# Two of four batches get their queries by rows of a block, turned by transposing transfers, with a second set of row-order tables

## The chip, the core and the metric

The kernel runs on one core of one Trainium2 chip. The metric is the device time of one execution in microseconds; the median of the runs shown is the time of the kernel. One execution was also profiled, and all rows below are of that one.

## What is computed

```python
# q, k, v: [4, 8, 768, 64]; sort_net: [4, 8, 8, 8]; w_ch1: [512, 2048]; w_ch2: [2048, 512]
for _ in range(5): P = exp(P - max); P /= P.sum(-1); P /= P.sum(-2)      # sinkhorn
k_sorted = einsum('bhij,bhjcd->bhicd', P, k_blocks)                      # 8 blocks of 96 tokens
v_sorted = einsum('bhij,bhjcd->bhicd', P, v_blocks)
attn = softmax(q_block @ k_sorted_block.T / 8)                           # inside a block
x = (attn @ v_sorted_block) as [4, 768, 512]
u = x + real(fft(fft(x, axis=1), axis=2))
un = (u - mean) / sqrt(var + 1e-6)
out = u + relu(un @ w_ch1) @ w_ch2                                       # "MLP"
```

## The kernel before

Four batches pass through the same stages. **Mix**: for each of four pairs of heads `hp`, queries and keys are loaded by POOL (`load_kq`; the transfer also turns them to 16 bits). Partition p of a loaded tile holds six neighbouring tokens, so a block's 96 tokens stand in an order of their own, `PERM`. TensorE turns the queries (`q_mix`: twelve matmuls with the identity, L800, and a copy out of PSUM to `qT` by DVE or ACT); twelve more mix the keys (`k_mix`, L821, evicted to `kz`). From batch 1 on the two sets are one step, `psQK`. The values are mixed (L761), written to `vo` and moved by SP to `vs` (`v_move`, L783).

**Attention**: per pair and half of the blocks `y`, scores (`products`, L853), a maximum or minimum on DVE, `exp` on ACT, then the product with the values (L937) and a division on DVE to `xr`. In batches 2 and 3 (`turned`) the probabilities come out with queries on the partitions and are turned by a transposing transfer on SP's queue (`turn_e`, L912), two per half.

**Fourier transform**: sums and differences of blocks (`fold`), a matmul with the tables `cse` and `cso` over the tokens of a block (`dft_s`, L983, L1005, out to `W`), a matmul over the model dimension (`dft_d`, L1045), and `residual` (L1088) with a selection matrix `rsel`. The rows of `cse`, `cso` and `rsel` stand in the order of the queries in a block. All three are loaded once, by SP.

**Norm and MLP**: `PQ`, `u`, statistics (L1115), `un`, transposes into `unT` (by TensorE in batch 0, L1162, by SP's transposing transfers later, L1153), then the MLP's matmuls: L1180 (`ph`, 128 groups of four) and L1198 (`pc`, 96 groups of four).

A planner, `Plan`, sets the order on every engine. Each step has a cost per engine, a due time (moved by the tables `LEAD` and `MOVE`) and, if it ends in a transfer, `work` and `hop`; `SPARE` is added to a transfer's landing. The order is fixed when the kernel is built: each engine runs its own list and waits where an input is late. Into gaps of TensorE's list before the planned time `FILL_END` it puts matmuls that nobody reads (`fill`, L687). Loads for batches 2 and 3 are held back by one-element copies on POOL (`landed`, L493), which wait for an earlier load.

Of the kernel before, what the change touches and what calls it, by code (L numbers as in the profile page):

```python
# [28 lines left out]
TURN = 8  # L29
# [31 lines left out]
def _consts():  # L61
# [21 lines left out]
    ss = BLK * np.arange(4)[None, :] + PERM[:, None]  # L83
# [39 lines left out]
    at = np.argsort(PERM)  # L123
# [84 lines left out]
class Plan:  # L208
    FORM_IN = dict(psQ=1, psK=1, psQK=1, psaT=1, psS=2, psRh=5, psM=6)
    FORM_OUT = dict(FORM_IN, psT=2)  # L210
    ENTER, LEAVE, STAY = 0, 95, 1e7
    ARRAY = dict(psQ=320, psK=320, psQK=640, psaT=53, psS=155, psA=213, psB=213, psT=395, psV=160, psN=159, psWo=510,
        psWe=271, psF=430, psR=324, psRh=162, psY=213, ph=640, pc=853, psG=640, psP=60, pcol=60)
    FILL_LOW, FILL_END, WINDOW = 1931, 49895, 3413
    LAG, PE_TAIL, MARGIN, NEAR = 45.0, 250.0, 120.0, 14.0
    PORT, PORT_WAIT = ("fold", "fold_d", "minus", "nm", "un", "xem", "kron"), 450.0
    OVER = {"V": 80, "A": 100}
    SPARE = 909
    REL = dict(cdh=38223, cse=17364, cso=12887, idx=43588, load_k2=82421, load_k3=45767, load_q1=32871,
        load_q2=83959, load_q3=155044, load_v1=26759, load_v2=99397, load_v3=18886, rsel=30643, w0=38071,  # L220
        w1=51566, w2=7303, w3=34666, w4=62534, w5=56660, w6=23527, w7=18919)
    LEAD = dict(P=(-10.9, -33.1, 10.8, 47.7), Q=(-21.5, 0, 0, -19.8), We=(-1.6, -0.2, 0.2, 0),
        Wo=(24.9, -10.8, 0, -20.3), a16=(-11.2, -16.6, 1.4, 0), a_out=(26.9, 10.9, 36.1, -20.1),
        add=(-68, 0, 74.6, -10.9), amr=(0.9, 2.6, 18, 0), amt=(-58.6, -2.5, -4.5, 0), const=(15.9, 0, 0, 0),
        exp=(10.9, 48.2, 35.7, -8.7), fold=(-27.1, -23.4, -64.4, 3.7), fold_d=(0, -4.8, 34.7, 0.1),
        hold=(-53, 0, 0, 0), kron=(2.5, 74.7, 2.1, 37.8), kz=(-20.2, 0.8, -52.6, -46.3),
        load_k16=(0, 75.7, 0, -47.8), load_q16=(0, 7.8, -23.1, -0.3), load_v=(0, 26.7, -51.4, -35.5),
        m8=(6.6, 0, 0, 0), max=(-79.4, -48, -32.6, -52.3), minus=(-40.1, -17.1, -9.6, -5.8),
        nm=(-1, -10.8, -13.3, 71.6), norm=(4.5, -39, -29.1, -35.3), ot=(43.5, 40.4, -18.7, 0),
        outt=(0, 0, -51.4, -37), patch=(3.2, 28.2, 5.1, -43.2), pc=(9.3, 0, 0, 0), pca=(19.5, 0, 0, 0),  # L230
        pcol=(-10, 0, 0, 0), pcs=(28.9, 0, 0, 0), ph=(83.6, 26, 3.3, -1.1), psA=(0, 2.4, 0, -26.9),
        psB=(7.1, 0, 2, 26.3), psF=(5.8, -0.3, 0, 19.8), psG=(71.5, 0, 0, 0), psK=(-31.8, 17.3, 37.2, 0.7),
        psM=(-45.2, 0, 0, 0), psN=(-18, -17.6, 7.4, 67), psP=(20.4, 0, 0, 0), psQ=(53.7, -3.6, 23.4, -2.4),
        psQK=(0, 8, 17.6, -16.7), psR=(-1.8, 58.2, 0, 1.6), psRh=(32.2, 16.3, 7.5, -22.1),
        psS=(47.1, 34.2, -65.3, -27.4), psT=(-29.9, -33.5, 0, 0), psV=(-64.4, 0, 24.7, -4.5),
        psWe=(-51.6, 33.5, 1.3, 0), psWo=(4.8, 37.8, 2.9, 0), psX=(26.8, 14.2, -8.8, 0), psY=(0, 25.5, 0, 0),
        psaT=(-0, -2.4, 10.7, 0.2), ptm=(-12.5, 0, 0, 0), qT=(-5.1, 0, 5.8, -57.3), relu=(1.5, 0, 9.6, 81.6),
        root=(0, 9.5, 9.1, -21.3), row_zero=(0, -26.2, -15.6, -2), stats=(-6.4, -23.2, -10.4, 1.7),
        store=(-1.5, 0, -29.6, 6.6), turn_e=(0, 0, 0, -18.6), turn_u=(0, 0, 26.1, 10.7),
        u=(37.5, 8.6, 31.2, -14.6), un=(48.6, 33.2, -20.3, -21.5), unT=(0, 62.4, 0, 15.1),  # L240
        v_move=(-23, 23.6, 0, 26.2), v_sum=(0, -10.6, 0.2, 43), vg=(65.5, 0, 0, 0),
        vo=(14.8, -41.4, -78.1, 0), weights=(62.6, 0, 0, 0), xem=(-20.9, -4.2, 0, -9),
        xom=(-38.7, 63.9, 0, 1.4))
    MOVE = dict(P={(1, 2): 15.5}, add={(2, 2): 0.8, (2, 4): 65.3, (3, 2): 44.7, (3, 4): 9.4},
        amt={(3, 0): -11.9}, const={(0, 3): -19.1},
        exp={(2, 1): 24.2, (2, 4): -13.7, (2, 5): -5.9, (2, 7): -1.2, (2, 15): -0.5, (3, 0): 6.4, (3, 5): -13.8},
        fold={(0, 3): -17.6, (0, 4): 32, (1, 3): -51.4, (2, 1): -8.6, (3, 4): 13.8}, fold_d={(2, 0): 41.8},
        kz={(3, 0): -12.5}, load_k16={(1, 1): 8.8}, minus={(3, 4): -45.6, (3, 7): -43.3}, nm={(1, 0): -20.1},
        norm={(0, 6): 6.2}, psN={(0, 4): -19}, psV={(3, 1): 0.8, (3, 2): -46.8, (3, 3): 0.9, (3, 7): -39.2},
        psWe={(0, 1): 13.5, (1, 0): 38.7, (1, 3): 15.6}, psY={(0, 2): 12.9}, relu={(0, 27): 2},  # L250
        stats={(1, 3): 41.9}, turn_e={(3, 0): 0.5}, u={(0, 2): -54.4}, un={(0, 5): -7.3},
        v_move={(1, 4): 3.2, (1, 8): 32.2, (2, 4): 2.7, (2, 6): 43.9, (2, 7): 8.4, (2, 8): 16.1, (2, 9): 44.8, (2, 11): 6.9},
        vo={(3, 0): 5.5, (3, 6): -24.1})
# [206 lines left out]
def kernel(  # L460
# [12 lines left out]
    nc.scalar.preload_act_table_set("natural_log_exp_and_others")  # L473
    names = ("small", "cdh", "cse", "cso", "vrow", "ones", "idx", "rsel")
    (small_d, cdh_d, cse_d, cso_d, vrow_d, ones_d, idx_d, rsel_d) = [
        nc.inline_tensor(a, name=n) for n, a in zip(names, _consts())]

    const = ctx.enter_context(tc.tile_pool(name="const", bufs=1))
    psum = ctx.enter_context(
# [892 lines left out]
    for b in range(B):  # L1372
        if b == 0:
            mix(0)
# [59 lines left out]
```

## Time and profile before

| | |
|---|---|
| median of 3 runs | 291.07 us (288.71 to 293.12) |
| the profiled execution | 291.53 us, span 289.7 us |
| TensorE busy | 276.1 us, 95% |
| VectorE, ScalarE, GpSimd busy | 66%, 63%, 42% |
| mean granted TensorE clock | 0.985 |
| bytes moved by transfers | 30.41 MB in 50847 packets |

The span runs from the first to the last instruction of the program. A start-to-start distance of two groups says more of TensorE than the busy time, since matmuls overlap and their ends are modelled.

### The profile page before, as it was taken

What the parts mean: (1) busy time and instruction counts of PE and PEld (TensorE: products, weight loads), DVE (VectorE), ACT (ScalarE), POOL (GpSimd) and SP (SyncE); (2) the same over time, 40 slices, a digit from 0 to 9 for tenths busy, and PEclk for the clock granted to TensorE, in tenths of its full rate; (3) what the DMA queues carried; (4) which work ended last, traced back from release to release, by engine and by line L of the source; (5) the groups of instructions that cost most, each with busy time, mean ns of one, the idle gap of its engine ahead of it and who ended that gap; (6) DMA issues with size and microseconds to landing.
All of it is one profiled execution on the core that took longest, in us unless ns stands there. A gap on an engine that the chain in (4) does not pass through costs nothing.

```text
span 289.7 us, 6877 instructions
## 1 busy us (share of the span) xinstructions
PE 276.1 (95%) x2598; PEld 161.9 (56%) x2598; DVE 191.5 (66%) x435; ACT 183.8 (63%) x455; POOL 122.0 (42%) x190
## 2 busy tenths in 40 slices
PE   7899999689999999999999999999999999999993
PEld 2467766257765565445555576455645645645541
DVE  6749988978797897673679998987866572001011
ACT  2368976778894779746495679788725832712700
POOL 8473736314226789765833256230023641112010
PEclk9979999979999999999999999999999999999998
DMA  7998969998856876969935862553311025002002
GB/s 101 182 162 169 154 106 163 185 140 136 107 88 104 112 147 96 124 143 186 130 88 113 154 112 38 115 144 75 70 38 38 36 54 129 36 34 77 1 36 74
DMA packets 50847, 30.41 MB, mean 105 GB/s; under 512 B 25962, under 2 KB 48900, under 8 KB 50812
## 3 DMA queue, kind: packets, MB, share of 16 engines
q0 software_dynamic: 19040, 19.40, 40.6%
q1 hardware_dynamic: 31574, 10.28, 18.9%
q8 instruction: 20, 0.33, 0.5%
q10 hardware_dynamic: 200, 0.30, 0.4%
q14 instruction: 13, 0.11, 0.2%
HBM read 28.50 MB, written 6.29 MB: 120 GB/s over the span
## 4 chain that ended last, share of the span: by engine, by line
PE 78%; DVE 14%; DMA 3%; issue 2%; ACT 1%; DVEq 0%
PE bank L1180 29%; PE bank L1198 24%; PE bank L983 3%; PE bank L853 3%; PE bank L937 3%; DMA eT<-es 2%; PE bank L1088 2%; PE bank L875 2%; PE bank L821 2%; PE bank L761 2%; PE bank L1005 1%; PE bank L800 1%; DVE st L1115 1%; PE bank L1045 1%; DVE mxs L863 1%
## 5 line engine op out<-in xcount | busy, mean ns | idle before, releaser
L1198 PE MATMUL bank<-w2sb,hr 128*128 128x512 f16 x384 | 90.0, 379 | 0.0
L1180 PE MATMUL bank<-unT,w1sb 128*128 128x384 f16 x512 | 89.2, 329 | 0.0
L1186 ACT ACTIVATE hr<-bank 128x384 f16<-128x384 f32 x128 | 60.7, 495 | 38.7 <-PE bank L1180 37.9
L1180 PEld LDWEIGHTS <-w1sb 128*128 128x128 f16 x512 | 49.1, 99 | 32.2 <-issue 1.5
L1219 POOL DMA_INDIRECT out_dram<-outt,idx_sb x22 | 22.6, 1026 | 88.5 <-DVE outt L1207 70.0
L1198 PEld LDWEIGHTS <-hr 128*128 128x128 f16 x384 | 36.0, 98 | 38.2
L1207 DVE SCALAR_TENSOR_TENSOR outt<-u,bank 128x512 f32<-128x512 f32 x24 | 16.4, 682 | 41.8 <-PE bank L1198 41.8
L892 ACT ACTIVATE sm<-bank,mns 96x96 f32<-96x96 f32 x128 | 32.3, 352 | 2.4 <-DVE mns L898 2.0
L944 DVE TENSOR_TENSOR xr<-bank,rz 96x512 f16<-96x512 f32 x32 | 22.0, 686 | 1.1
L547 ACT CAST W<-bank 128x384 f16<-128x384 f32 (+1 forms) x38 | 12.8, 380 | 12.9 <-PE bank L983 8.5
L1115 DVE BATCH_NORM_STATS2 st<-u 128x6 f32<-128x512 f32 x24 | 16.4, 681 | 4.0 <-POOL u L1101 3.9
L863 DVE TENSOR_REDUCE mxs<-bank 96x8 f16<-96x768 f32 x16 | 14.5, 949 | 5.6 <-PE bank L853 5.5
L1100 POOL TENSOR_TENSOR u<-u,PQ 128x257 f32<-128x257 f32 x18 | 12.8, 711 | 9.9 <-DVE PQ L1058 8.6
L898 DVE TENSOR_REDUCE mns<-bank 96x8 f32<-96x768 f32 x16 | 15.0, 944 | 2.6 <-PE bank L853 2.2
L1101 POOL TENSOR_TENSOR u<-u,PQ 128x255 f32<-128x255 f32 x18 | 12.6, 699 | 3.6 <-DVE PQ L1058 3.6
L908 ACT ACTIVATE es<-sm 96x384 f16<-96x384 f32 x19 | 10.0, 528 | 6.1 <-DMA eT<-es 5.8
L880 ACT ACTIVATE sm<-bank 96x768 f32<-96x768 f32 x16 | 12.8, 801 | 1.4 <-PE bank L853 1.2
L922 ACT ACTIVATE eT<-sm 96x768 f16<-96x768 f32 x16 | 13.4, 841 | 0.4
L569 POOL DMA_DIRECT2D k<-in_k_dram x15 | 11.0, 733 | 5.9 <-PE bank L821 4.8
L937 PEld LDWEIGHTS <-eT 97*128 97x128 f16 (+1 forms) x256 | 11.2, 101 | 3.8 <-ACT eT L922 0.5
L943 DVE RECIPROCAL rz<-bank 96x8 f32<-96x8 f32 x32 | 6.3, 197 | 10.6 <-PE bank L937 10.5
L983 PE MATMUL bank<-cso_sb,xso 120*128 120x384 f16 (+1 forms) x64 | 13.1, 326 | 0.0
(144 smaller groups left out, 426.5 us busy)
## 6 DMA issues: line engine op xcount, KB each, us to landing
vs<-vo SPq DMA_DIRECT2D x48, 65.0 KB
v<-in_v_dram POOLq DMA_DIRECT2D x16, 192.0 KB, 4.9
k<-in_k_dram POOLq DMA_DIRECT2D x15, 192.0 KB, 5.5
q<-in_q_dram POOLq DMA_DIRECT2D x15, 192.0 KB, 4.1
w1sb<-in_moe_w_ch_dram POOLq DMA_DIRECT2D x4, 512.0 KB, 8.0
w2sb<-in_moe_w_ch_dram POOLq DMA_DIRECT2D x4, 512.0 KB, 5.9
eT<-es SPq DMA_TRANSPOSE x32
cdh_sb<-cdh SPq DMA_DIRECT2D x1, 387.0 KB
```

Of the source, the lines that this page charges most:

```text
L863: ("max", b, {"V": 945}, lambda e: nc.vector.tensor_reduce(mxs[n].t.rearrange("p (t j) -> p t j", t=2), pair(pS, BLK), axis=AX.X, op=ALU.max),
L892: nc.scalar.activation(sm.t[:, i], pair(pS, BLK)[:, t, i % 4], AF.Exp, bias=mn.t[:, i:i + 1], scale=-1.0)
L898: ("max", b, {"V": 945}, lambda e: nc.vector.tensor_reduce(mn.t.rearrange("p (t j) -> p t j", t=2), pair(pS, BLK), axis=AX.X, op=ALU.min), ...
L937: nc.tensor.matmul(ps[0:wide(i).stop - BLK * i, i // 4, i % 4], et[0:97, wide(i)], vs[b % 2][:, 4 * y + i % 4, (D + 1) * h:(D + 1) * (h + 1)])
L944: nc.vector.tensor_tensor(xr2[b % 2][0:BLK, 4 * y:4 * y + 4, 128 * hp:128 * hp + 128].rearrange("p j (t d) -> p t j d", t=2), ps[:, :, :, ...
L983: nc.tensor.matmul(ps, x[0:n, j], cso[0:n, j, :], start=(j == 0), stop=(j == 3))
L1115: nc.vector.bn_stats(st.t, us[b, i, m].t)
L1180: nc.tensor.matmul(ps, w1sb[:, mc, 128 * fc:128 * fc + 128], unT[b, gr].t[:, mc, :], start=(mc == 0), stop=(mc == 3))
L1186: nc.scalar.activation(dst, bank(pH, [128, 384]), AF.Relu)
L1198: nc.tensor.matmul(ps, hr[f4].t[:, fc % 4, 128 * t:128 * (t + 1)], w2sb[:, fc, :], start=(fc == 0), stop=(fc == 15))
L1207: step("outt", b, {"V": 687}, lambda e, u=u, pC=pC, o=o: nc.vector.scalar_tensor_tensor(o.t, u.t, RSC, bank(pC, [128, DM]), op0=ALU.mult, ...
L1219: step("store", b, {"G": 1050}, lambda e: nc.gpsimd.indirect_dma_start(out=out.rearrange("b s m -> (b s) m"), out_offset=bass.IndirectOffs ...
```

## The change

For batches 2 and 3 the queries of one head are loaded as `[96 rows, 8 blocks, 64]`, so that a partition is a row of every block. Two loads fill one tile of a pair of heads, and runs of 64 elements take the place of runs of 384. Two transposing transfers on SP's queue (`turn_q`) then make `qT`; the twelve matmuls and the copy out of PSUM are gone there, and `psQK` is split. A block's queries are now in plain order in these batches, so `cso`, `cse` and `rsel` are overwritten by a second set, made with the plain order, when batch 1 has been done with them. The tile `q16` grows from 768 to 1024 elements a partition, and the ring `v16` loses one of its six tiles. `TURN` now counts batches and says the same as before.

```diff
+QT = 2
-    ENTER, LEAVE, STAY = 0, 95, 1e7
+    ENTER, LEAVE, STAY = 0, 95, 58161
-    FILL_LOW, FILL_END, WINDOW = 1931, 49895, 3413
-    LAG, PE_TAIL, MARGIN, NEAR = 45.0, 250.0, 120.0, 14.0
+    FILL_LOW, FILL_END, WINDOW = 1852, 63588, 3413
+    LAG, PE_TAIL, MARGIN, NEAR = 45.0, 250.0, 120.0, 9.0
-    SPARE = 909
+    SPARE = 630
...
-    LEAD = dict(P=(-10.9, -33.1, 10.8, 47.7), Q=(-21.5, 0, 0, -19.8), We=(-1.6, -0.2, 0.2, 0),
+    LEAD = dict(P=(-9.4, -14.6, 25.1, 1.7), Q=(0.5, 0, -0.1, 9.3), We=(25.2, -21.8, 0, 2.5),
...
-    ring("q16", 3, [128, 2, G * D], F16)
-    ring("v16", 6, [128, 2, G, D], F16)
+    ring("q16", 3, [128, NB, 128], F16)
+    ring("v16", 5, [128, 2, G, D], F16)
...
+            if b >= QT and tag == "q16":
+                for hh in range(2):
+                    step("load_q16", b, {"G": 850}, lambda e, t=d[b, hp], hh=hh: nc.gpsimd.dma_start(
+                        t.t[0:BLK, :, D * hh:D * hh + D],
+                        q[b, hs.start + hh].rearrange("(i r) d -> r i d", r=BLK)),
+                        w=[(d[b, hp], hh)], work=1500, hop=1750, bulk=2 if b > 1 else 1, need=need, rel=f"load_q{b}")
+                continue
...
+        if b >= QT:
+            for t in range(2):
+                step("turn_q", b, {"S": 1300}, lambda e, t=t: nc.sync.dma_start(
+                    qT[b, hp].t[:, 384 * t:384 * t + 384].rearrange("x (i r) -> x i r", r=BLK),
+                    q16[b, hp].t[0:BLK, 4 * t:4 * t + 4].rearrange("q i x -> q (i x)"), transpose=True),
+                    r=[(q16[b, hp], 0), (q16[b, hp], 1)], w=[(qT[b, hp], t)], work=800, hop=900)
+            return
...
+        if b == QT:
+            for key, t, d in (("cso", cso, cso2_d), ("cse", cse, cse2_d), ("rsel", rsel, rsel2_d)):
+                step("const", b, {"S": 530}, lambda e, t=t, d=d: nc.sync.dma_start(t, d.ap()),
+                     w=[key], work=6 * int(np.prod(t.shape)) // 1000 + 50, hop=1500, bulk=True, need=125e3)
```

All entries of `REL`, `LEAD` and `MOVE` are new as well, so the order changes on every engine. Over the whole program TensorE loses 96 matmuls of L800 and gains ten unread ones (18 in place of 8). Three places matter below.

**SP, from batch 1's last row copy to batch 2's first probabilities.** `qT` is the turned queries, `eT` the turned probabilities. Before:

```order
L752 DMA xr_184<-xr_184 1x16x224
L752 DMA xr_184<-xr_184 1x16x32
L912 DMA_TRANSPOSE eT_145<-es_100 128x4x96
L912 DMA_TRANSPOSE eT_146<-es_102 128x4x96
L912 DMA_TRANSPOSE eT_145<-es_101 128x4x96
```

Now:

```order
L770 DMA xr_183<-xr_183 1x16x32
L826 DMA_TRANSPOSE qT_85<-q_74 128x4x96 x2
L1402 DMA cso_sb<-cso 120x1536
L1270 DMA idx_sb<-idx 128x24
L826 DMA_TRANSPOSE qT_86<-q_75 128x4x96 x2
L1402 DMA cse_sb<-cse 120x772
L939 DMA_TRANSPOSE eT_144<-es_99 128x4x96
```

Four turns of queries and two tables stand ahead of the first turned probabilities; the third table (`rsel`) stands between later ones.

**DVE, the norm of batch 0** (`PQ` is the spectrum, `u` the sum, `st` its statistics; `vo`, `amr`, `amt`, `xso` and `xse` here are batch 1's mix). Before, from the first spectrum:

```order
L863 TENSOR_REDUCE mxs_94<-bank 96x8
L1058 TENSOR_TENSOR PQ_114<-bank,ot_113 128x258 x2
L1100 TENSOR_TENSOR u_116<-bank,PQ_114 128x257
L1101 TENSOR_TENSOR u_116<-bank,PQ_114 128x255
L1115 BN_STATS st_129<-u_116 128x6
```

Now:

```order
L558 CAST amr<-bank 128x512
L726 CAST amt<-bank 128x4x16
L727 TENSOR_TENSOR amt<-bank,amt 128x4x8
L558 CAST xso<-bank 24x4x128
L1085 TENSOR_TENSOR PQ_113<-bank,ot_112 128x258 x2
L738 COPY xse<-xso 24x8x128
L790 SCALAR_TENSOR_TENSOR vo<-a_193,bank 128x6x64 x3
L1127 TENSOR_TENSOR u_115<-bank,PQ_113 128x257
L1128 TENSOR_TENSOR u_115<-bank,PQ_113 128x255
L790 SCALAR_TENSOR_TENSOR vo<-a_193,bank 128x6x64 x2
L1085 TENSOR_TENSOR PQ_114<-bank,ot_112 128x258 x2
L1142 BN_STATS st_128<-u_115 128x6
```

Five `vo` and five small steps of batch 1 moved ahead of batch 0's statistics; they stood behind them before.

**ACT, the last batch's norm** (`ot` is the copy of an odd spectrum, `rstd` belongs to the norm; each `hr` evicts one group of four L1180 matmuls of batch 2's MLP, so its count tells how many such groups TensorE has there). Before:

```order
L547 COPY ot_113<-bank 128x258
L1186 ACTIVATE hr_66<-bank 128x384
L1075 COPY PQ_114<-bank 1x516
L1186 ACTIVATE hr_66<-bank 128x384
L1186 ACTIVATE hr_67<-bank 128x384 x4
L1186 ACTIVATE hr_68<-bank 128x384
L547 COPY ot_113<-bank 128x258
```

Now (the copies `ot` are on DVE):

```order
L1102 COPY PQ_114<-bank 1x516
L1213 ACTIVATE hr_68<-bank 128x384 x2
L1213 ACTIVATE hr_69<-bank 128x384 x3
L1151 ACTIVATE rstd_131<-mv_125,epst 128x2
L1152 ACTIVATE rstd_131<-rstd_131 128x2
L1213 ACTIVATE hr_69<-bank 128x384
```

From batch 3's first spectrum to batch 3's first MLP matmul TensorE had 16 such groups of L1180 before and has 8 now; beside them stood 13 groups of L1198 before, and stand 12 now and eight matmuls of `residual`.

107 lines of the change are left out of this document (59 added, 48 removed).

## The prediction

> **What bounds the kernel now.** I read the page first: busy time, the share of the chain that ended last, and the costliest groups.
>
> ```profile
> span 289.7 us, 6877 instructions
> ...
> PE 276.1 (95%) x2598; PEld 161.9 (56%) x2598; DVE 191.5 (66%) x435; ACT 183.8 (63%) x455; POOL 122.0 (42%) x190
> ...
> PE 78%; DVE 14%; DMA 3%; issue 2%; ACT 1%; DVEq 0%
> ...
> L1198 PE MATMUL bank<-w2sb,hr 128*128 128x512 f16 x384 | 90.0, 379 | 0.0
> L1180 PE MATMUL bank<-unT,w1sb 128*128 128x384 f16 x512 | 89.2, 329 | 0.0
> ```
>
> TensorE carries 78% of the chain, and no matmul of the MLP ever waited (idle 0.0 in both groups). An average hides stages, so next comes the table of windows of 10 us (busy time and count of PE, PEld, DVE, ACT, POOL, then the granted clock, the share of the transfer engines, GB/s).
>
> ```profile
> 50.00:60.00 10.00, 6.13 (x59) 3.69 (x58) 9.61 (x29) 7.02 (x16) 4.04 (x7) 0.96 1.06 161
> 60.00:70.00 10.00, 9.86 (x151) 6.60 (x150) 7.68 (x16) 7.74 (x15) 2.99 (x4) 0.87 0.89 133
> 100.00:110.00 10.00, 9.55 (x112) 5.95 (x111) 9.45 (x18) 8.35 (x24) 8.81 (x16) 1.00 0.83 146
> 120.00:130.00 10.00, 9.43 (x71) 4.61 (x70) 7.13 (x15) 5.16 (x18) 6.47 (x11) 1.00 0.71 141
> 250.00:260.00 10.00, 10.00 (x55) 5.13 (x53) 0.69 (x1) 3.49 (x8) 0.97 (x1) 1.00 0.00 0
> ```
>
> The two halves differ. Up to 60 us TensorE has gaps and DVE is the full engine (9.61 of 10 in 50 to 60); from the first MLP matmul on TensorE is full, with 0.14, 0.45 and 0.57 us idle in the three rows between. So the end is the time of the first MLP matmul, plus all matmul work that is left then, plus waits. An edit pays only by moving one of these three.
>
> **The transposes that go.** The order of time on TensorE shows a `psQK` step: L800 turns queries, L821 mixes keys.
>
> ```profile
> 101.17 0.53 PE L800 MATMUL bank<-ident,q 128*64 128x128 f16 x12
> 101.53 0.50 PE L821 MATMUL bank<-kron,k 128*64 128x128 f16 x12
> 101.87 0.50 PE L800 MATMUL bank<-ident,q 128*64 128x128 f16 x12
> 102.20 0.50 PE L821 MATMUL bank<-kron,k 128*64 128x128 f16 x12
> ```
>
> From start to start twelve L800 take 0.36 us (101.53 − 101.17). The busy figure, 0.53, would count the overlap twice. Eight steps go: 8 × 0.36 = **2.9 us off** a full engine, all gained. The eight copies to `qT` (on DVE or ACT) go too; I value them at nothing, since these engines are 66% and 63% busy and TensorE's MLP work covers their stages.
>
> **The ten more unread matmuls.**
>
> ```profile
> L687 PE MATMUL bank<-junk 128*128 128x512 f16 x8 | 2.6, 383 | 0.0
> ```
>
> At 0.383 us each they cost 3.8 us at most, if no gap were there. They stand ahead of 64 us of planned time, where 50 to 60 us alone had 3.87 us idle: I take nothing. They do buy clock. Rows of the chain with eight L1180 each:
>
> ```profile
> 60.70 2.27 PE bank L1180 x8
> ...
> 76.68 1.30 PE bank L1180 x8
> ```
>
> The first eight MLP matmuls took 2.27 us at a reduced clock, against 1.30 later; the window 60 to 70 was granted 0.87, that is 1.3 us of full clock lost, and 50 to 60 another 0.4, in which TensorE was partly idle. The low clock follows the window in which TensorE was busy 6.13 of 10. If the unread matmuls keep it busy, this comes back: bounds 0 (another window turns slow) to −1.7, and I take **−1.3**.
>
> **The first MLP matmul comes later.** DVE now does batch 1's five `vo`, `amr`, `amt` (two steps), `xso` and `xse` ahead of batch 0's statistics. Their prices, by form, and the gaps in DVE's order of time in the same stretch (bracketed):
>
> ```profile
> L772 DVE SCALAR_TENSOR_TENSOR vo<-a,bank 128x384 f16<-128x384 f16 x24 | 11.8, 549 | 0.5 <-PE bank L761 0.4
> L551 DVE CAST xso<-bank 24x512 f16<-24x512 f32 x2 | 1.4, 696 | 0.7 <-PE bank L713 0.7
> L720 DVE COPY xse<-xso 24x1024 f16<-24x1024 f16 x3 | 1.3, 423 | 0.4 <-ACT xso L547 0.4
> L551 DVE CAST a<-bank 128x512 f16<-128x512 f32 x1 | 0.7, 691 | 0.6 <-PE bank L695 0.6
> L708 DVE CAST amt<-bank 128x64 f16<-128x64 f32 x4 | 0.9, 219 | 0.6 <-PE bank L701 0.6
> L709 DVE TENSOR_TENSOR amt<-bank,amt 128x32 f16<-128x32 f32 x4 | 0.8, 191 | 0.1
> ```
>
> ```profile
> 43.46 1.82 DVE L863 TENSOR_REDUCE mxs<-bank 96x8 f16<-96x768 f32 x2 [0.99 <-PE bank L853]
> ...
> 46.95 0.43 DVE L1100 TENSOR_TENSOR u<-bank,PQ 128x257 f32<-128x257 f32 x1 [1.00 <-PE bank L1088]
> ...
> 49.02 0.76 DVE L1058 TENSOR_TENSOR PQ<-bank,ot 128x258 f32<-128x258 f32 x2 [0.36 <-ACT ot L547]
> ```
>
> The sum is 5 × 0.549 + 0.691 (`amr`, by the cast of the same form) + 0.219 + 0.191 + 0.696 + 0.423 = 5.0 us. The gaps hold 0.99 + 1.00 + 0.36 = 2.35 us. So the first MLP matmul comes 2.6 us (all gaps used) to 5.0 us (none) later; the middle is 3.8. Against that, TensorE now does two pairs of L800 and L821 ahead of it that stood behind it, 2 × 0.70 = 1.4 us from start to start (101.87 − 101.17), and batch 1's four short L713, together about 1.6 us of work that is no longer left then. Net +1.0 to +3.4, and I take **+2.2**.
>
> **What the transfers take.** Both queues as the page has them: packets, MB, share of 16 engines' span.
>
> ```profile
> q0 software_dynamic: 19040, 19.40, 40.6%
> q1 hardware_dynamic: 31574, 10.28, 18.9%
> ...
> q<-in_q_dram POOLq DMA_DIRECT2D x15, 192.0 KB, 4.1
> ```
>
> A q0 packet took 0.406 × 16 × 289.7 us / 19040 = 99 ns at 1019 bytes on average, a q1 packet 28 ns at 326 bytes. A pair's queries were 256 runs of 768 bytes as written; they become two loads of 768 runs of 128 bytes. One engine of 16 then needs, for a pair, 1536 / 16 × 28 to 99 ns = 2.7 to 9.5 us, against 256 / 16 × 99 = 1.6 us. Nearest in size is the q1 packet, so I take 2.7: eight pairs add 9 us of transfer time in the 120 us around batches 2 and 3. That alone is hidden, since the share there stood at 0.71 to 0.83 in the rows above and TensorE has MLP work meanwhile. POOL issues eight loads more, each under the 1 us that its issues take here, with 42% of it busy: nothing.
>
> The page "DMA: Bandwidth & Descriptors" of the Trainium skill (Specifications) says that transfers under 512 B make the engine read, modify and write. If that doubled the 28 ns, an estimate would be 5.3 us a pair, not 2.7; the average q1 packet here, at 326 bytes, shows no such price, and no row has a load in runs of 128 bytes. If it held, the second rival below would gain from it.
>
> **What waits in SP's queue.** SP issues 16 transposing transfers and three tables more. Where it is dense, the order of time shows this:
>
> ```profile
> 192.99 16.50 SPq L912 DMA_TRANSPOSE eT<-es  x11
> ```
>
> Eleven back to back in 16.50 us are 1.50 us each: SP sets the pace there. Two turns of queries now stand among batch 3's thirteen last ones, and behind each a turn of probabilities waits, and then L937. The tables wait for batch 1's last matmuls that read the old ones; behind them stand the turns of batch 2's probabilities. How late a turn can be, and how near the end is to its inputs, the chain and DVE's order show:
>
> ```profile
> 114.33 6.55 DMA eT<-es
> ...
> 218.49 1.96 PE bank L1088 x10
> 220.45 0.46 PE bank L1045 x8
> 220.91 0.86 PE bank L1198 x4
> ...
> 243.69 10.40 PE bank L1180 x64
> ```
>
> ```profile
> 241.91 0.55 DVE L1141 TENSOR_SCALAR un<-u,mv,rstd 128x512 f16<-128x512 f32 x1 [0.95 <-DMA unT<-un]
> ```
>
> One turn landed 6.55 us after its issue, and TensorE's MLP work hid it. At the end 23.2 us of other work (243.69 − 220.45) covered the way from batch 3's first spectrum to its first MLP matmul, and the fourth transpose, which that matmul needs, landed at 241.9: 1.8 us to spare. The cover now has eight groups of L1180 less (8 × 0.65 = 5.2 us), one group of L1198 less (0.9) and eight L1088 more (8 × 0.196 = 1.6): 4.5 us less. The way itself is also ordered anew, so the wait there is 0 to 4.5 − 1.8 = 2.7 us. With waits like those of 100 to 130 us (0.45 + 0.57) added once, the bounds are 0 to +3.7, and I take **+1.5**, below the middle, since the order lets ACT make three of the four `un` that DVE made in between other work.
>
> **Sum.** 291.53 − 2.9 − 1.3 + 2.2 + 1.5 = 291.0 us for a profiled execution. The profiled one stood 0.46 above the median of the runs shown, so the prediction is **290.6 us**. With the bounds of its terms (−2.9, −1.7 to 0, +1.0 to +3.4, 0 to +3.7) the likeliest case spans 287.5 to 295.3.
>
> **Rival 1, faster: the head does not get longer.** DVE's work of batch 1 falls into its gaps and into waits that the order no longer has, so the first MLP matmul comes at 60.7 us as before and 1.6 us less is left then. For it: TensorE itself stood idle 3.87 us in 50 to 60. Against: DVE was busy 9.61 of 10 in that row. Price: −2.9 − 1.7 − 1.6, and the 1.2 us idle in the three rows after 60 us vanish: −7.4, so 283.7 us by the median.
>
> **Rival 2, slower: SP's queue becomes the bound of batches 2 and 3.** Queries reach `qT` through POOL's serial loads (two per pair where one stood, each followed by a wait for an earlier one), two turns on SP, and only then come scores. For it: 1.50 us per turn in the dense stretch, a turn that took 6.55 us, `SPARE` cut from 909 to 630 ns, the cover at the end cut by 4.5 us. Against: 23 us of pure MLP cover and a TensorE list that hid all of this so far. It decides once a turn lands later than the MLP work planned ahead of its reader. Price: two more turns in the dense stretch of each batch, 2 × 2 × 1.50 = 6.0, and 2.7 at the end, on −2.9 − 1.3 + 2.2 = −2.0: +6.7, so 297.8 us.
>
> **How the numbers follow.** The likeliest case gets 0.46, rival 1 0.25, rival 2 0.29. A measurement of this kernel tells about 2% from no change (5.8 us: 285.2 to 296.9); rival 1 lies below, rival 2 above, and edges pass to and fro: faster 0.24, within 0.47, slower 0.29. The range of 8 in 10 reaches to the middle of both rivals: 283.0 to 298.5.
>
> **What would show it.** L800 with 96 matmuls fewer, and L1180 never idle. The first L1180 starts at 63 to 65 us, not 60.7, and eight of them take 1.3 us, with a granted clock of 1.00 in 60 to 70. From 130 to 230 us TensorE idles under 2 us. If it idles more, with L937 or L853 waiting for `eT` or `qT`, rival 2 is right; if the first L1180 starts by 61 us, rival 1 is. A single load in rows landing past 6 us would break the 2.7 us a pair.

## The result: 3.5% slower, not the same

The changed kernel took 301.0 us (median of 4 runs, 298.62 to 307.0) against 290.63 us (288.71 to 293.12): ratio 1.035, 95% interval 1.025 to 1.046. The prediction was 290.6 us, 283.0 to 298.5. The profiled execution took 298.62 us. An execution over 1.5% above the fastest of its kernel is kept out of the ratios below, and since the profiles of e1, e9, e11, e12 and e13 (experiments further down) are of such executions, they are read for places and not for sizes.

The page of the changed kernel (L1207 and L1225 are now the MLP's matmuls):

```profile
span 296.6 us, 6753 instructions
...
q0 software_dynamic: 29408, 19.40, 45.3%
...
PE 70%; DMA 13%; DVE 10%; ACT 2%; issue 2%; SPq 1%; POOL 0%; DVEq 0%; POOLq 0%; ACTq 0%
...
L1207 PE MATMUL bank<-unT,w1sb 128*128 128x384 f16 x512 | 89.6, 327 | 0.0
...
q<-in_q_dram POOLq DMA_DIRECT2D x16, 96.0 KB, 3.9
```

TensorE's share of the chain fell from 78% to 70%, and transfers' share rose from 3% to 13%; the MLP's first matmuls themselves still never waited (idle 0.0). Where that lies is read from one group, the first matmuls of the MLP (minimum/median/maximum ns, then the first and the last start), first of before, then of the change.

```profile
L1180 PE MATMUL bank<-unT,w1sb x512: 323/326/524, 60.5 to 274.5; 128*128 128x384 f16 x171
```

```profile
L1207 PE MATMUL bank<-unT,w1sb x512: 323/326/457, 67.6 to 281.5; 128*128 128x384 f16 x171
```

The first starts 7.1 us later, and from the first to the last it is 214.0 us before and 213.9 us now. So the whole 7.1 us of the profiled time stand ahead of the MLP; behind its start, 2.9 us of transposes are gone and about 1.6 us of other matmul work has moved ahead, and yet that length is the same: something else took as long. The windows show what (busy time and count of PE, PEld, DVE, ACT, POOL, then the granted clock, the share of the transfer engines, GB/s), and under them stand TensorE's waits from 130 to 230 us (sum, times, longest):

```profile
50.00:60.00 10.00, 6.95 (x55) 3.88 (x53) 9.77 (x27) 2.85 (x7) 0.94 (x2) 1.00 1.13 183
60.00:70.00 10.00, 8.61 (x97) 5.29 (x96) 8.78 (x21) 7.97 (x16) 1.98 (x3) 0.66 0.73 108
150.00:160.00 10.00, 9.26 (x104) 5.06 (x102) 7.01 (x16) 6.99 (x24) 6.42 (x12) 1.00 0.87 160
160.00:170.00 10.00, 8.62 (x87) 5.00 (x84) 8.34 (x22) 5.58 (x14) 2.94 (x6) 1.00 1.12 85
210.00:220.00 10.00, 8.70 (x79) 4.85 (x80) 7.98 (x19) 4.98 (x17) 1.24 (x2) 1.00 0.38 86
```

```profile
PE bank L964 <- DMA eT<-es: 2.1, 2, 1.4
PE bank L1010 <- DVE xso L987: 1.4, 1, 1.4
PE bank L1032 <- DVE xse L992: 0.2, 1, 0.2
```

TensorE, full in these stages before (10.00, 9.94 and 10.00 there), idles 3.4 us in the last three rows. The waits listed are 3.7 us: 2.1 for turned probabilities, and 1.6 for two folds. Of these, the fold of 1.4 stood on DVE behind a step that itself waited 1.76 us for a turn; the one of 0.2 was not followed back. The clock granted from 60 to 70 us is 0.66, not the 1.00 that was forecast.

Ahead of the MLP the order of time on DVE carries the delay. Two rows of before (first and fourth statistic of batch 0), then five of the change:

```profile
47.74 0.69 DVE L1115 BATCH_NORM_STATS2 st<-u 128x6 f32<-128x512 f32 x1
...
54.14 0.69 DVE L1115 BATCH_NORM_STATS2 st<-u 128x6 f32<-128x512 f32 x1
```

```profile
43.10 1.81 DVE L890 TENSOR_REDUCE mxs<-bank 96x8 f16<-96x768 f32 x2
44.83 0.41 DVE L987 TENSOR_TENSOR xso<-xr 96x512 f16<-96x512 f16 x1
46.62 0.56 DVE L558 CAST W<-bank 128x384 f16<-128x384 f32 x1 [1.39 <-ACT eT L949]
...
54.70 0.68 DVE L1142 BATCH_NORM_STATS2 st<-u 128x6 f32<-128x512 f32 x1
...
60.19 0.69 DVE L1142 BATCH_NORM_STATS2 st<-u 128x6 f32<-128x512 f32 x1
```

The first statistic is 7.0 us late, the fourth 6.0. Batch 0's last fold (L987) now stands behind batch 1's two maxima (1.81 us), and the cast to `W` behind the fold and a wait of 1.39 us. `W` is what the first spectrum of batch 0 reads, on TensorE (L1035 before, L1062 now):

```profile
43.75 0.38 PE L1035 MATMUL bank<-cdh_sb,W 128*128 128x258 f16 x2
```

```profile
47.67 0.38 PE L1062 MATMUL bank<-cdh_sb,W 128*128 128x258 f16 x2
```

It comes 3.9 us later. The same matmuls read a second thing, the table `cdh`. SP issues its load 9.8 us later than before, because in the new order it stands behind two copies of batch 0's row, which wait for a fold:

```profile
33.55 0.36 SPq L1243 DMA_DIRECT2D cdh_sb<-cdh  x1
```

```profile
43.34 0.59 SPq L1270 DMA_DIRECT2D cdh_sb<-cdh  x1
```

So the first spectrum has two bounds: `W`, whose cast ends at 47.2 us, and close before it the table; e18 below shows when the table lands.

After the fourth statistic the chain of work that ended last runs through batch 1 again:

```profile
64.24 0.78 PE bank L818 x9
65.02 0.64 PE bank L846 x12
...
66.20 0.78 PE bank L818 x10
66.98 0.64 PE bank L846 x12
67.62 0.88 PE bank L1207 x4
```

The two pairs of L818 and L846 that were moved ahead of the MLP took 2.84 us there (0.78 + 0.64, twice), in the window with the clock of 0.66. Up to the first MLP matmul the delay is then 3.9 us at the first spectrum, 6.0 at the fourth statistic and 7.1 at the end.

### The profile page after: what moved, and what is told of

The parts are those of the page before. It is cut to its first block, busy times and chain, and to the rows that moved or that the text cites. A ratio compares the mean times of both kernels' runs of the same rounds, so it can differ in the third digit from the quotient of the medians.

```text
span 296.6 us, 6753 instructions
## 1 busy us (share of the span) xinstructions
PE 279.3 (94%) x2512; PEld 161.0 (54%) x2512; DVE 186.6 (63%) x436; ACT 185.3 (62%) x446; POOL 129.7 (44%) x205
## 3 DMA queue, kind: packets, MB, share of 16 engines
q0 software_dynamic: 29408, 19.40, 45.3%
## 4 chain that ended last, share of the span: by engine, by line
PE 70%; DMA 13%; DVE 10%; ACT 2%; issue 2%; SPq 1%; POOL 0%; DVEq 0%; POOLq 0%; ACTq 0%
PE bank L1207 27%; PE bank L1225 22%; DMA eT<-es 7%; DMA vs<-vo 4%; PE bank L880 3%; PE bank L964 2%; PE bank L1115 2%; PE bank L1010 2%; DVE xr L971 2%; DMA q<-in_q_dram 2%; PE bank L1072 2%; PE bank L846 1%; DMA xr<-xr 1%; ACT sm L919 1%; PE bank L902 1%
## 5 line engine op out<-in xcount | busy, mean ns | idle before, releaser
L1207 PE MATMUL bank<-unT,w1sb 128*128 128x384 f16 x512 | 89.6, 327 | 0.0
L1225 PE MATMUL bank<-w2sb,hr 128*128 128x512 f16 x384 | 88.2, 380 | 0.0
L1213 ACT ACTIVATE hr<-bank 128x384 f16<-128x384 f32 x128 | 60.6, 493 | 33.2 <-PE bank L1207 32.8
L1207 PEld LDWEIGHTS <-w1sb 128*128 128x128 f16 x512 | 48.2, 98 | 31.5 <-issue 0.5
L1225 PEld LDWEIGHTS <-hr 128*128 128x128 f16 x384 | 36.2, 98 | 39.9
L554 ACT CAST W<-bank 128x384 f16<-128x384 f32 (+1 forms) x31 | 11.2, 393 | 10.4 <-PE bank L1032 6.0
L964 PE MATMUL bank<-vs,eT 97*128 97x65 f16 (+1 forms) x256 | 13.2, 199 | 3.8 <-DMA eT<-es 2.1
L964 PEld LDWEIGHTS <-eT 97*128 97x128 f16 (+1 forms) x256 | 11.8, 103 | 8.0 <-DMA eT<-es 3.0
L1165 ACT ACTIVATE un<-u,nm,rstd 128x512 f16<-128x512 f32 x14 | 11.2, 811 | 7.8 <-DMA unT<-un 4.1
L599 POOL TENSOR_TENSOR vh<-v 128x384 f32<-128x384 f16 x12 | 11.3, 942 | 7.8 <-DMA v<-in_v_dram 7.5
L937 DVE TENSOR_SCALAR es<-sm 96x384 f16<-96x384 f32 x15 | 7.4, 494 | 10.1 <-DMA eT<-es 6.8
```

The costliest lines, as they stand in the source:

```text
L964: nc.tensor.matmul(ps[0:wide(i).stop - BLK * i, i // 4, i % 4], et[0:97, wide(i)], vs[b % 2][:, 4 * y + i % 4, (D + 1) * h:(D + 1) * (h + 1)])
L1207: nc.tensor.matmul(ps, w1sb[:, mc, 128 * fc:128 * fc + 128], unT[b, gr].t[:, mc, :], start=(mc == 0), stop=(mc == 3))
L1213: nc.scalar.activation(dst, bank(pH, [128, 384]), AF.Relu)
L1225: nc.tensor.matmul(ps, hr[f4].t[:, fc % 4, 128 * t:128 * (t + 1)], w2sb[:, fc, :], start=(fc == 0), stop=(fc == 15))
```

## Experiments

Two kinds of edit were used. In e1 to e4 the planner ran again, with other numbers or steps. In the others (e7 apart, which changes only how a load reads) its choice was replaced by a list of all steps in the order of their emission, taken from the kernel before or from the changed one. One thing differs besides what is named: the planner still put in the unread matmuls by its own times, 18 in the change, e6 and e8, but 22, 25, 28 and 28 in e9, e10, e17 and e18. The diffs of lists are shown in short form:

```diff
     def run(self):
         self.began = True
         self.order()
...
+        for i, line in enumerate(ORDER.split()):
+            name, b, k, e = line.split(",")
+            s = by.pop((name, int(b), int(k)))
...
+            self.emit(s, e, t)
```

### Numbers and mechanism apart, by the planner

**e1**, the numbers alone (`-QT = 2`, `+QT = 4` in the changed kernel):

> The changed kernel's numbers for the order, without its mechanism: all queries are loaded and transposed as before, no second tables. On every engine the order up to the first MLP matmul is that of the changed kernel. Theory (the order of the head costs the time): the first L1207 starts at 67 to 68 us as in the changed kernel (67.55) and not at 60.5; the 96 transposes are back (+2.9 us), and of the waits for eT in batches 2 and 3 (about 4 us) some go: 296 to 301 us. Rival (row loads, turns and tables cost it): the first L1207 at 60.5 to 62 us and 289 to 293 us.

**e2**, the mechanism with the old numbers (`STAY`, `FILL_LOW`, `FILL_END`, `NEAR`, `SPARE`, `REL`, `LEAD` and `MOVE` of before):

> The whole mechanism of the change with the numbers for the order that the kernel before has (no numbers for the new turns). Up to the first MLP matmul every engine's order is that of before. Theory (order of the head): the first MLP matmul at 60 to 61 us; then 2.9 us of transposes less and 0 to 5 us of new waits: 288 to 293 us. Rival (the mechanism costs it): 296 us or more, with the time lost between 100 and 230 us on waits for qT, eT or the tables.

**e3**, the old numbers for batches 0 and 1, the new ones for 2 and 3 (`LEAD = b[:2] + a[2:]`, and `MOVE` likewise):

> The change with its own numbers for batches 2 and 3, and the old ones for batches 0 and 1 and for the planner's general constants. Up to the first MLP matmul the order is that of before. Theory: the first MLP matmul at 60 to 61 us, and the waits for transfers in batches 2 and 3 stay as in the changed kernel (about 4 us from 130 to 230 us): 298.6 - 7.1 + 1.7 (work that was moved ahead is back behind) = 293 us, 290 to 296. Rival (the mechanism): 297 us or more.

**e4**, the second load of tables alone, in the kernel before:

```diff
+        if b == 2:
+            for key, t, d in (("cso", cso, cso_d), ("cse", cse, cse_d), ("rsel", rsel, rsel_d)):
+                step("const", b, {"S": 530}, lambda e, t=t, d=d: nc.sync.dma_start(t, d.ap()),
```

> The kernel before, and its own three tables loaded a second time at the place where the change loads the new ones. The orders of TensorE, DVE and ACT stay those of before. Theory: three more issues on SP and under 1 MB more, hidden by the MLP: no difference, under 1 us. Rival (the second load holds up SP's turns behind it, or the readers of the tables): 2 to 4 us more, with waits of psWo, We or psR for the tables.

Measured: e1 309.2 us, ratio 1.057 (1.048 to 1.066); e2 326.5 us, 1.117 (1.105 to 1.130); e3 319.5 us, 1.096 (1.084 to 1.108), though its fastest run was 313.36 us; e4 293.66 us, 1.008 (1.005 to 1.012). e1 came out slower than its theory's 296 to 301 us. In e2 and e3 the first MLP matmul came at 60.2 and 58.9 us, as expected, and yet they were the slowest: my theories missed, and the times lie where the rivals had them, only further out. TensorE's waits (e2, then e3) name the places:

```profile
PE bank L1203 <- DMA unT<-un: 19.6, 2, 12.4
```

```profile
PE bank L844 <- DMA qT<-q: 12.3, 1, 12.3
```

In e2 the wait was for a transpose of the MLP's own input, which the rival had not named. In e3 a turn of queries itself was 12.3 us late: it stood in SP's queue behind moves of values and other turns. That is rival 2's mechanism, in an order that was not made for it. The second load of tables alone costs 1.3 to 3.5 us by its interval, not nothing.

### Two heads and two rests

**e5**, the list of before up to the ninth group of the MLP, then the changed kernel's; **e6**, the reverse:

```diff
-ORDER = changed
+ORDER = before[:ninth ph] + [s for s in changed if s not in before[:ninth ph]]
```

> The change, with the order replayed from two lists: on every engine the kernel before's order up to its ninth group of L1180, and from there what is left in the changed kernel's own order. (The two lists contain almost the same steps up to that place.) Theory (the new order of the head costs 7 us, and the waits of batches 2 and 3 are the change's own): the first MLP matmul at 60 to 61 us instead of 67.55, about 1.7 us of matmul work back behind it, waits from 130 to 230 us as in the changed kernel: 298.6 - 7.1 + 1.7 = 293 us, 290 to 295.5. Rival (the late head is only where a loss of the transfers shows; started earlier, TensorE waits longer for transfers in batches 2 and 3): 297 us or more, with over 8 us idle from 130 to 230 us.

> The reverse: the kernel before (queries by TensorE, no second tables), with the changed kernel's order up to its ninth group of L1180 and the kernel before's own order from there. Theory: the first MLP matmul at 67 to 68 us, 1.7 us of matmul work less behind it, and all of the rest as before: 291.5 + 7.1 - 1.7 = 297 us, 295 to 299. Rival (the head's order alone costs little): 63 us or earlier and at most 293.5 us.

e5, the old head on the new rest, took 301.66 us, 1.033 (1.022 to 1.045): nothing won. e6, the new head on the old rest and without the mechanism, took 298.82 and 294.66 us, two values and too few for an interval. First and last of the MLP's first matmuls in e5, then in e6:

```profile
L1378 PE MATMUL bank<-unT,w1sb x512: 323/326/528, 59.4 to 284.3; 128*128 128x384 f16 x171
```

```profile
L1349 PE MATMUL bank<-unT,w1sb x512: 323/326/337, 69.4 to 281.8; 128*128 128x384 f16 x171
```

The new head delays the MLP whatever follows, and the old rest behind it takes 212.4 us, 1.6 less than before, the work moved ahead. But behind the old head the new rest takes 224.9 us, 11 more. The rival of that run had the time, and waits for transfers as its cause, but not their place: from 130 to 230 us TensorE idled 2.9 us, not over 8, and from 80 to 100 us it idled 6.6. In e5, the wait from 70 to 100 us, POOL's order of time there, and the window after:

```profile
PE bank L1017 <- DMA k<-in_k_dram: 6.6, 3, 5.6
```

```profile
78.47 0.70 POOL L758 DMA_DIRECT2D k<-in_k_dram  x1 [0.33 <-issue]
...
87.76 0.77 POOL L671 COPY landed<-w2sb 1x1 f16<-1x1 f16 x1 [6.58 <-DMA w2sb<-in_moe_w_ch_dram]
```

```profile
90.00:100.00 10.00, 7.25 (x50) 3.70 (x50) 1.75 (x4) 3.25 (x6) 4.54 (x11) 0.67 0.88 90
```

Batch 2's keys are loaded behind the last weights, one load waiting for another to land. In e5 these four loads were issued at 78.5, 79.3, 88.5 and 93.5 us; in the change, with its late head, at 72.0, 72.9, 83.8 and 89.4. So the splice gave POOL a later order for them. In the window with the wait for keys the clock is granted at 0.67. When the keys are read shows in the group of L821 (before, from 80 us) and of L846 (the change, from 80 us):

```profile
L821 PE MATMUL bank<-kron,k x48: 219/219/219, 93.3 to 117.1; 128*64 128x128 f16 x48
```

```profile
L846 PE MATMUL bank<-kron,k x48: 219/219/243, 87.7 to 94.2; 128*64 128x128 f16 x48
```

Before, TensorE mixed them 32.8 us after the first MLP matmul and later; now it does 20.1 us after it. Behind an MLP that starts at 60 us the new rest would want the four pairs of keys from 80 to 87 us; in e5 they were mixed at 82.6, 83.5, 92.0 and 97.9.

Two runs test this: **e12** moves the key loads of e5 ahead of weights in POOL's queue, **e15** takes the mechanism out of e5.

```diff
-... weights 0 7, load_k16 2 0, load_k16 2 1, weights 0 4, load_k16 2 2 ...
+... load_k16 2 0, load_k16 2 1, weights 0 7, load_k16 2 2, weights 0 4 ...
```

> The kernel of the old head spliced to the new rest, with POOL's queue alone changed: the first two loads of batch 2's keys stand ahead of the seventh weight load, the third ahead of the eighth. Theory (in that kernel the 7 us won in the head were lost to the load of keys at 86 us behind two weight loads, 5.7 us, and to the lower clock after it, 0.67 from 90 to 100): that wait falls under 1 us, the clock stays at 1.00, and 301.1 - 5.7 - 3 = 292.5 us, 290.5 to 295. Rival (the loads are the bound as a whole, and another one is late instead): L1225 or L1207 waits for w2sb, or psK for the next keys, for 4 us or more; 297 us or more.

> The old head spliced to the new rest, as in the earlier kernel, without the mechanism (queries loaded as before and transposed by TensorE, no second tables). Theory (the new rest reads batch 2's keys 26 us after the first MLP matmul, and behind an old head they cannot have come by then, with or without the mechanism): TensorE waits for k at 84 to 88 us for 3 us or more again, 298 to 304 us. Rival (the row loads or SP's turns made the keys late): that wait falls under 1 us, 292 to 295 us.

e12 took 306.25 us, 1.052 (1.045 to 1.059), slower than e5: by its time the rival was right, this order of the loads does not help. Its profile shows the four key loads at 78.7, 79.9, 87.7 and 100.0 us, on the whole no earlier than in e5, so keys that come early were not tried by it. e15 took 305.64 us, 1.042 (1.033 to 1.052), and waits for k as long without any row load or turn:

```profile
PE bank L1009 <- DMA k<-in_k_dram: 6.2, 2, 4.8
```

So the late keys belong to the splice of the two orders and not to the mechanism, and in that splice the early head was worth nothing. e12's profile still has TensorE waiting for k, as its rival said. No run here had the old head, the new rest and keys that came in time.

### The mechanism in either order

These decide between order and mechanism: the same list of steps, with only the queries' steps exchanged. **e13**, the mechanism in the old order, its loads and turns placed by hand; **e16**, the same placed better:

```diff
-... psQK 2 0, qT 2 0, kz 2 0 ...
+... load_q16 2 0, load_q16 2 1, turn_q 2 0, turn_q 2 1, psK 2 0, kz 2 0 ...
```

> The whole mechanism in the kernel before's own order, replayed as a list: TensorE's order is that of before without the 96 transposes, DVE's and ACT's without the eight copies; POOL issues two row loads where one load of queries stood (batch 2's first two pairs ahead of or right behind the first keys, batch 3's first two some 20 us earlier), and the 16 turns stand in SP's queue where their rows have landed. Theory (the order, not the mechanism, made the changed kernel slower): 291 - 2.9 + 0 to 3 of waits and second tables = 288 to 292 us, the first MLP matmul at 60 us, no wait for qT over 2 us. Rival (the mechanism itself costs it): 296 us or more, with waits for qT or eT of over 6 us in sum from 85 to 230 us.

> The mechanism in the kernel before's own order as before in the run of the change in the old order, with the row loads and turns moved out of the way of the three waits that it showed: in POOL's queue the third pair's row loads of batch 2 stand behind the residual adds, the fourth's behind batch 2's sums of values, batch 3's first two pairs' behind batch 3's sums; in SP's queue batch 3's turns stand behind the row for the mean and, three pairs of them, behind the moves of values. TensorE, DVE and ACT as there. Theory (place, not mechanism): the waits of psR for the patch (4.7 us at 100), of the sums (8.5 us at 154) and of psR for xr (5.7 us at 184) go, 290 to 296 us. Rival (the queues are simply too full: the waits turn up elsewhere, for qT, eT or k): 300 us or more.

**e14**, the new order without the mechanism (a `psQ` and a `qT` step at each pair's second turn, no `const` of batch 2):

> The changed kernel's own order, replayed as a list, without its mechanism: queries loaded as before, transposed by TensorE (12 matmuls a pair, one copy on DVE) at the place of a pair's second turn, no second tables. Theory (the order): 298 to 302 us, as the changed kernel: 2.9 us of transposes come back, and 0 to 4 us of waits for eT go. Rival (the mechanism): 294 us or less.

| | without the mechanism | with it |
|---|---|---|
| old order | 1 (290.6 us) | 1.079 (1.069 to 1.090), placed better 1.048 (1.043 to 1.053) |
| new order | 1.048 (1.041 to 1.054), 304.4 us | 1.035 (1.025 to 1.046), 301.0 us |

By this table the new order costs most. Without the mechanism it costs 13 us, and its first MLP matmul comes at 70.5 us (e14):

```profile
L1359 PE MATMUL bank<-unT,w1sb x512: 322/326/528, 70.5 to 286.4; 128*128 128x384 f16 x171
```

From the first to the last it is 215.9 us against 213.9 with the mechanism: there the mechanism seems worth 2.0 us of the 2.9 of its transposes, by one profile each, and the intervals of the two times overlap. The rest of the difference is in the head, 70.5 against 67.6 us, and its cause is not known: e8, below, has the same order of steps on TensorE, DVE and ACT as e14, and its MLP begins at 66.9 us. So part of the 13 us may be this difference of some 3 us. In the old order the mechanism costs 14 us even after its loads were moved out of the way. What TensorE waited for in e13, and in e16:

```profile
PE bank L890 <- POOL vg L772: 8.5, 3, 5.2
PE bank L1286 <- DMA xr<-xr: 5.9, 2, 5.5
PE bank L1286 <- ACT PQ L1273: 4.6, 1, 4.6
```

```profile
PE bank L1447 <- ACT PQ L1342: 4.1, 1, 4.1
PE bank L959 <- POOL vg L841: 2.2, 1, 2.2
```

The first three are other work of POOL and SP standing behind row loads and turns: sums of values, a copy of the row for the mean, and residual adds (ACT's PQ waited for POOL's `u`). In e16 POOL's `u` was still the cause of the 4.1 us, as ACT's row shows, with that residual add standing behind batch 3's row loads:

```profile
181.72 0.58 ACT L1342 COPY PQ<-bank 1x516 f32<-1x516 f32 x1 [4.50 <-POOL u L1368]
```

Moving the loads and turns alone brought the ratio from 1.079 to 1.048, some 9 us. No TensorE, DVE or ACT step moved between these two.

### Parts of the mechanism in the new order

**e7**, long runs (`q[b, h].rearrange("(r i) d -> r (i d)")`, which reads the same bytes and leaves out their right arrangement); **e8**, turns by TensorE (8 matmuls and a copy a pair); **e11**, half of batch 2's moves of values on ACT's queue (`plan.engines[e].dma_start`):

> The changed kernel, where each load of queries in batches 2 and 3 takes the same bytes in 96 runs of 1024 bytes instead of 768 runs of 128 bytes; the queries then stand in another order, so this kernel computes something else. Every engine's order is unchanged. Theory (the short runs cost transfer time that is hidden): 298 to 301 us as the changed kernel, waits for eT from 130 to 230 us unchanged at about 4 us. Rival (short runs clog the transfer engines and delay the turns of probabilities): those waits fall under 1.5 us, 296 us or less.

> The changed kernel in its own replayed order, with the 16 turns of queries taken out of SP's queue: the rows are loaded as in the change and turned by TensorE (8 matmuls of 96x96 per pair) with one copy on DVE at the place of a pair's second turn. Theory (16 turns in SP's queue make the turns of probabilities late): waits from 130 to 230 us fall from 4.0 to under 1.5 us, TensorE gets 8 x 0.2 = 1.6 us more work: 295 to 298 us. Rival (those waits come from elsewhere, the order or the row loads): the waits stay and the time is 299 to 301 us.

> The changed kernel in its own replayed order; of the twelve moves vs<-vo of batch 2, six are issued on ACT's queue instead of SP's. Theory (SP's queue is the bound in batch 2: twelve moves, a turn of queries and ten turns of probabilities back to back): the block of ten turns starts 3 to 4 us earlier than 146.1, the waits of L964 for eT at 152.9 and 162.7 us (2.1 us) go, and the time falls by 1.5 to 2 us, to 297. Rival (the turns wait for probabilities, or ACT pays for the issues): the block starts at 145.5 or later or the waits stay over 1.5 us; 298.5 to 301.

e7: 298.8 and 297.46 us, no difference that two values can show; TensorE's waits from 130 to 230 us were 2.6 us (1.2 for `eT`, 1.4 for a fold) instead of 3.7. e8: 299.4 us, 1.025 (1.014 to 1.036), between theory and rival: the waits fall from 3.7 us to 2.5, not to 1.5.

The queue and the loads in e7, then the waits in e8 from 130 to 230 us:

```profile
q0 software_dynamic: 18656, 19.40, 39.7%
...
q<-in_q_dram POOLq DMA_DIRECT2D x16, 96.0 KB, 2.7
```

```profile
PE bank L1127 <- DMA eT<-es: 1.5, 1, 1.5
PE bank L1195 <- DVE xse L1155: 0.5, 1, 0.5
PE bank L1173 <- DVE xso L1150: 0.5, 1, 0.5
```

A load in long runs lands after 2.7 us instead of 3.9, and q0 took 39.7% of 16 x 295.9 us for 18656 packets, against 45.3% of 16 x 296.6 us for 29408: 270 us less for 10752 packets less, 25 ns each. e11: 301.14 us, 1.024 (1.014 to 1.034), which does not tell its two theories apart.

What is left waits for SP's block of turned probabilities, in the changed kernel:

```profile
138.91 5.78 SPq L801 DMA_DIRECT2D vs<-vo  x9
144.73 1.26 SPq L826 DMA_TRANSPOSE qT<-q  x1
146.09 17.89 SPq L939 DMA_TRANSPOSE eT<-es  x10
```

Ten turns take 17.89 us; before they took 16.53 from 139.70. A query turn of 1.26 us stands right ahead of the block, which starts 6.4 us later than before.

### The head by pieces

In the new order: **e9**, batch 0's last fold put first; **e10**, batch 1's nine DVE steps behind five statistics; **e17**, behind the whole norm; **e18**, e9 and e17 together. The edit of e10, on the list:

```diff
-... amr 1 0, amt 1 0, psB 1 0, xom 1 0, psV 1 0, vo 1 0 ... stats 0 0 ... stats 0 4 ...
+... stats 0 0 ... stats 0 4, psaT 1 0, amr 1 0, amt 1 0, psB 1 0, xom 1 0, psV 1 0, vo 1 0 ...
```

> The changed kernel in its own replayed order, with one edit in the head: batch 0's last fold (L987), the matmuls that read it (L1010, the last L1022 group, L1062) and their casts stand ahead of batch 1's first two maxima on DVE, of its score matmuls on TensorE and of its exponentials on ACT, as they do in the kernel before. Theory (3.9 of the 7 us come from batch 1's maxima, 1.8 us, and the wait behind them, ahead of batch 0's last fold): the first L1062 at 44 to 45 us instead of 47.7, the first MLP matmul at 63 to 65 us instead of 67.55. Rival (the nine steps of batch 1 ahead of the statistics hold it up whatever comes before): the first MLP matmul within 1 us of the changed kernel's. If what starts earlier is not lost again, the time falls as much, to 295 to 296 us; if batch 2's loads then end last, TensorE waits for k between 85 and 100 us and the time stays at 298 to 301.

> The changed kernel in its own replayed order, with the other edit in the head: batch 1's vo, amr, amt, xso and xse on DVE, with the matmuls that feed them and the cast on ACT, stand behind the fifth statistics of batch 0 instead of ahead of the first. Theory (these steps, 5.0 us of DVE, cost what the gaps do not hold): the first MLP matmul 2.5 to 5 us earlier than 67.55, at 62.5 to 65. Rival (they fill gaps that are there anyway): 66.5 or later. For the time the same holds as for the kernel with the last fold first: 294 to 296 us, or 298 to 301 if batch 2's loads end last.

> The changed kernel in its own replayed order; batch 1's amr, amt, xso, xse and vo on DVE and the matmuls that feed them stand behind all six statistics of batch 0 and behind the transposes of its fourth normalized tile. Theory (these 5.0 us of DVE cost 3 of the 7 us): fourth statistic at 56 us instead of 60.2, first MLP matmul at 63 to 65 us instead of 67.55. Rival (something else holds it): 66 us or later. The time itself may stay at 298 to 301 us, since the spliced kernel with the old head won nothing.

> The same, and batch 0's last fold with its matmuls and casts ahead of batch 1's first two maxima. Theory (the maxima and the wait behind them cost the other 4 us): first L1062 at 43.5 to 45 us instead of 47.7, first MLP matmul at 59.5 to 61.5 us. Rival: within 1.5 us of the kernel with the norm alone moved. The time, again, 298 to 301 us if the loads of batch 2 then end last; 292 to 295 if not.

The times were 1.031 (1.018 to 1.044), 1.032 (1.024 to 1.041), 1.030 (1.019 to 1.042) and 1.040 (1.024 to 1.056): all as the changed kernel. What e9's edit does in size is read from e18, which holds it too. In e10 the fourth statistic came at 56.1 us instead of 60.2, as expected, but the first MLP matmul stayed at 67.4: the step between root and normalization (`nm`) still stood behind the nine. In e17:

```profile
L1367 PE MATMUL bank<-unT,w1sb x512: 323/326/337, 70.6 to 284.2; 128*128 128x384 f16 x171
```

Now the last transpose that the MLP needs was issued at 62.9 us, 2.7 us earlier than in the changed kernel (65.6), and the MLP still began later, at 70.6 us (71.1 in e18): on TensorE, batch 1's mix of values (L939) and then two pairs of L978 and L1006 stand ahead of it, and the pairs wait for the `vo` steps that DVE now does late. In e10, e17 and e18 alike, the nine steps or what reads them stood before the MLP, on DVE or on TensorE. The first spectrum came at 46.6 us in e18, 1.1 us earlier and not 3 to 4, though the last fold was ready early (it started at 42.45 us). What held it there is the table `cdh`:

```profile
46.62 0.38 PE L1222 MATMUL bank<-cdh_sb,W 128*128 128x258 f16 x2 [0.44 <-DMA cdh_sb<-cdh]
```

SP issued that load at 43.34 us in e18, as in the changed kernel. So with the load issued there the first spectrum could not come before about 46.6 us, 2.9 us later than before, however early the last fold was, and e18 can't say what the maxima cost. No run moved this load alone. Which single step sets the head stays open.

## Why the prediction was wrong

- **The model held as bookkeeping.** Time of the first MLP matmul, work left then, waits: 7.1, -4.5 (2.9 and 1.6) and, by difference, +4.4 us make 7.0; the profiled executions differ by 7.1 (298.62 and 291.53). TensorE's list of waits names 3.7 of the 4.4.
- **The first MLP matmul: the step that failed.** Predicted 3.8 us later (2.6 to 5.0), measured 7.1. The prediction counted DVE's moved steps between the first spectrum and the statistics, and these came out small: 2.1 us by the fourth statistic, 3.1 by the first. But it put two other terms at nothing. It took the time of the first spectrum as unchanged, and that came 3.9 us later (43.8 to 47.7): the cast to `W` waited behind batch 1's maxima, and the table `cdh` was issued 9.8 us later on SP, an order that the prediction did not look at. And it counted the two pairs of query and key work as 1.4 us that leave the rest, but not as time in TensorE's way ahead of the MLP, where they took 2.84 us in the window with the clock of 0.66; this is in the last 1.0 us of the delay (3.9, 2.1 and 1.0). In five profiles with this head unedited (the change, e6, e7, e8, e14) the MLP began at 66.1 to 70.5 us; with the old one (before, e2 to e5, e16) at 58.9 to 60.5, and in e15 at 63.8. Which of the table, the maxima and the wait for `W` sets the first spectrum alone was not separated.
- **The clock, -1.3 us, did not come back.** TensorE was busy 6.95 of 10 in 50 to 60 us, despite ten more unread matmuls, and the grant from 60 to 70 us fell to 0.66, which is 3.4 us of full clock lost there. So the step that failed is that these matmuls would keep it busy and the clock with it. That gaps alone bring the low clock is not shown either: in e17 TensorE was busy only 8.52 and 6.34 of 10 from 50 to 70 us, and the clock stayed at 1.00 from 40 to 100.
- **The transposes, -2.9 us, were right in size** and lost in waits. Within the new order 2.0 us of it seem to be left from first to last MLP matmul, by one profile each (e14 and the change).
- **Waits, +1.5 us (0 to 3.7): too low.** They came to about 4.4 by difference, 3.7 in the list of waits, for `eT` and for folds, one of which stood behind a turn. That is rival 2's place, but spread over three stages and not at the end. With the query turns out of SP's queue (e8) the list holds 2.5 us.
- **"POOL issues eight loads more: nothing" was wrong** in another order: there (e13, e16) residual adds and sums of values behind those loads held up TensorE, and 6.3 us of it (4.1 and 2.2) were left in e16. In the new order the table of numbers had put the key work 12.7 us earlier after the MLP's start (20.1 for 32.8); whether that is what made room for the turns was not tested.
- **Row loads were priced rightly**: 25 ns a packet by the difference above, up to 34 if the 1536 long packets that replace them cost the average of 99 ns; 28 was taken. The page "DMA: Bandwidth & Descriptors" of the Trainium skill (Specifications) has transfers under 512 B read, modified and written; no doubling shows in these numbers.
- **Tables loaded twice** were given no term of their own; alone, in the old order, they cost 0.8%.
- **Rival 2's 297.8 us** was near the time by luck: its sum had 8.7 us of waits, of which at most 4.4 came, and a head later than its sum had, with the clock that did not come back, made up the rest.

What stays open: what the first spectrum would gain if the table `cdh` were loaded early in the new order, why the head of e14 is 3.6 us later than that of e8, and whether some other order would let the mechanism pay. No kernel tried here beat the one before.

## What to carry to other kernels

A change of mechanism together with a new order is two changes: replay each order with and without the mechanism before saying which one costs. In an order that fits tightly, a part of it has no price of its own; an early start is worth nothing if what follows waits for loads that come no earlier, so ask of the first consumer behind the moved point when its data land. Where a forecast starts its count at some step, ask first whether that step itself moves, and go through every engine's order for it, the queue that loads its tables too. Count work that is moved ahead of a bound at both places, as gone behind it and as added before it, at the clock of the place where it goes.

## What the runs showed of the hardware

The granted clock was low near TensorE's gaps in several profiles: 0.66 from 60 to 70 us in the change, e6 and e8 (0.68 in e7), 0.67 from 90 to 100 us in e5, with a wait of 5.6 us for keys. It was not so in all: in e17 it stayed at 1.00 through two windows busy 8.52 and 6.34 of 10. Loads in runs of 128 bytes, as written, cost the transfer engines 25 to 34 ns a run and landed 1.2 us later than the same bytes in 1024-byte runs (3.9 against 2.7 us). A transposing transfer of queries held SP's queue for 1.2 to 1.3 us, as long as two moves of values (0.64 us each); in a row of ten or eleven turns of probabilities it was 1.5 to 1.8 us each.
